# Strassen's products for the first four tiles of a pair's last phase, and the next batch's attention one step sooner there

## The chip, the cores and the metric

The kernel runs on one core of one Trainium2 chip. The metric is the device time of one execution in microseconds. In what follows PE is the TensorE engine with its matmuls, PEld its weight loads, DVE VectorE, ACT ScalarE, POOL GpSimd, and SP the engine that issues most of the transfers. Each of these works through its own instructions in the order in which the program wrote them.

## The reference

An attention block comes first. For 8 batches, 8 heads, 512 tokens and 32 state rows of 64 numbers each, it lets the tokens read from the states and the states read from the tokens. Its output, 544 rows of 512 numbers for each batch, goes through a feed-forward block with a cosine gate. Everything is float32.

```python
scores = scale * np.matmul(x, state.transpose(0, 1, 3, 2))
a = softmax(scores)                       # written out in the reference
xread = np.matmul(a, state)
scores2 = scale * np.matmul(state, x.transpose(0, 1, 3, 2))
a2 = softmax(scores2)
sread = np.matmul(a2, x)
x = concat([xread, sread], axis=2)        # to (4352, 512)
h = x @ w_in                              # 512 -> 2048
g = h * np.cos(h)
out = g @ w_out                           # 2048 -> 512
```

## The kernel before

**Tiles and steps.** The work is cut into tiles of 128 hidden units by 512 tokens: 16 tiles for each of 8 batches, and 16 more for the state rows at the end. A tile is one step of the loop at the end of the kernel function. The reads of the tokens are never formed: each batch's states are multiplied into `w_in` first (`products`, which PE writes to the PSUM tiles `at` and ACT copies to `sw`, L445), and the hidden values of a tile are then two products of 512 columns with the normalised weights `aT` (`hidden`, L471).

**Pairs and phases.** Two batches make a pair, and the product with `w_out` for a pair is done with Strassen's scheme over four phases. Phases 0 and 1 are the two halves of the 16 tiles of the even batch, phases 2 and 3 those of the odd batch. In phases 2 and 3 every tile also needs differences of `g` blocks (`sums`, `sums2`, L586): one for each tile on DVE, and in phase 3 two more on POOL. `output` (products at L624) follows a tile by three steps (`LAG`). In phase 3 it has four products of 512 columns for a tile, in phases 0 to 2 two, plus those that are left over from the pair before (`p7`, `p4`).

**Strassen in the hidden layer.** From batch 2 on, a predicate `seven` (L479) says for which tiles the hidden values of two neighbouring tiles are made together by seven products of 256 columns, in place of four products of 512 columns. `hidden_a` (four products, L514) is issued in the odd step before the pair, `hidden_b` (three products) in the pair's even step. Both take two fresh PSUM tiles `h` from a pool that has two. After `hidden_a`, ACT copies a part to the tile's place in `g_all` (L536), and DVE adds the rest (`sums_a`, L544 to L546). After `hidden_b` DVE adds again (`sums_b`, L559 and L560). The operands are differences that DVE makes once for each batch (`halves`, L493, to `aS`) and POOL for each pair of tiles (`sw_sums`, L509, four operations, to `swS` and into `sw`).

**The gate.** Every tile goes through four operations: `gate` (L567, ACT), `gate2` (L570, DVE), `gate3` (L573, ACT, a sine) and `gate4` (L580, DVE). A plain tile keeps its PSUM tile `h` until `gate4`. A tile made by Strassen's products leaves PSUM with the sums, and its gate reads `g_all`.

**The next batch's attention.** `plan(b)` writes down at which of the 16 steps of a batch each part of the next batch's attention goes in. `early` places the scores and row maxima (`scores` on PE, L319; `max1` on DVE, L333), their spread and the shift (L339, L356), the second maxima (`max2`, L349) and the exponentials (`exps` on ACT: L360 and twice L365, with a load of the activation table before and, at the next sine, after them), the sums (L333, L375, L376), their spread (L339), and the normalisation (`norm1`, L386). `late` places the turning of the weights (L392, copied by L397) and the reads (`reads`, L409). In the main loop a step's entries come in a fixed order: `hidden_b` and its sums, the next pair's `hidden_a`, go(0) (PE), `gate` and `gate2`, `sums_a`, go(1) and go(3) (the `x_` lists), `gate3`, `sw_sums`, `gate4`, the differences, go(2) and go(4) (the `y_` lists), and then the outputs. `exps` is in the list of go(4), so it stands at the end of its step on ACT.

Of the kernel before, what the change touches and what calls it, by code (L numbers as in the profile page):

```python
# [21 lines left out]
def kernel(  # L22
# [44 lines left out]
    NH = NF // 2  # L67
# [409 lines left out]


    def seven(t):  # L479
        return t.pair is not None and t.b > 1 and t.phase < 3  # L480

# [352 lines left out]
    def plan(b):  # L836
        pe, x_act, y_act, x_dve, y_dve = [
            {s: [] for s in range(NF)} for _ in range(5)]

        def prod(s, b, nt, *bank):  # L840
            pe[s].append((b, "products", nt) + bank)
            if b == 1 and 0 < nt < 3:
                x_dve[s].append((b, "products_taken", nt) + bank)
            else:
                x_act[s].append((b, "products_kept", nt) + bank)

        def pairs(s, b, name, kept, i):
            pe[s] += [(b, name, i), (b, name, i + 1)]
            x_act[s].append((b, kept, i))
            y_act[s].append((b, kept, i + 1))  # L850

        def early(b, s):
            if b == 1:
                pairs(s[0], b, "tokens", "tokens_kept", 0)
                pairs(s[1], b, "tokens", "tokens_kept", 2)
            else:
                for k in range(NK):
                    to = (x_dve, y_dve)[k % 2]
                    to[s[k // 2]].append((b, "tokens_turned", k))
            pe[s[2]].append((b, "scores"))  # L860
            x_dve[s[2]].append((b, "max1"))
            x_dve[s[3]].append((b, "spread1"))
            y_dve[s[3]].append((b, "shift"))
            x_dve[s[4]].append((b, "max2"))
            y_act[s[4]].append((b, "exps"))
            x_dve[s[5]].append((b, "sums"))
            y_dve[s[5]].append((b, "spread1"))
            x_dve[s[6]].append((b, "norm1"))

        def late(b, s):  # L870
            pairs(s[0], b, "turn", "turn_kept", 0)
            pe[s[1]].append((b, "reads", 0))
            pe[s[2]].append((b, "reads", 1))
            x_dve[s[2]].append((b, "keep"))
            if len(s) > 3:
                turned(b, s[3])

        def turned(b, s):
            pe[s].append((b, "keep2"))
            x_act[s].append((b, "keep3"))  # L880


        if b == 0:
            pe[0].append((0, "products", 0, SIDE, HC, WC))
            y_dve[0] += [(0, "products_taken", 0, SIDE, HC, WC),
                         (0, "inverse2")]
            prod(7, 0, 2, SIDE)
            prod(11, 0, 3)
            prod(13, 1, 0, MAIN)
            late(0, (1, 2, 3, 4))  # L890
            early(1, (5, 6, 7, 8, 9, 10, 11))
            late(1, (12, 13, 14))
        else:
            bank = (SIDE,) if b == 1 else ()
            if b == 1:
                turned(1, 0)
            prod(0, b, 1, *[MAIN for _ in bank])
            prod(4, b, 2, *bank)
            prod(9, b, 3, *bank)
            if b + 1 < B:  # L900
                prod(13, b + 1, 0)
                early(b + 1, (1 + (b == 1), 2 + (b == 1), 5, 6, 7, 8, 9))
                late(b + 1, (10, 11, 12, 15))
        return pe, x_act, y_act, x_dve, y_dve

# [21 lines left out]
    for step, t in enumerate(all_tiles):  # L927
        s = step % NF
        if s == 0 and t.b < B:
            steps = plan(t.b)  # L930
# [12 lines left out]
        if seven(t):  # L943
            if t.f % 2 == 0:
                hidden_b(t)
                sums_b(t)
                if s == NF - 2 and seven(all_tiles[step + 2]):
                    halves(t.b + 1)
        elif step != 1:
            hidden(t)  # L950
        first = len(ahead) > 1 and seven(ahead[0]) and ahead[0].f % 2 == 0
        if first:
            if not seven(t):
# [96 lines left out]
```

## Time and profile before

| what | us |
|---|---|
| median of 3 runs | 765.45 |
| lowest and highest of them | 764.82, 768.66 |
| profiled execution, own time | 765.96 |
| span in its profile | 764.2 |
| PE busy | 751.7 |
| DVE busy | 520.3 |
| ACT busy | 316.3 |
| POOL busy | 249.3 |

The span runs from the first to the last instruction of the profiled execution; what lies around it is the 1.8 us up to its own time. The granted TensorE clock is 0.997 of full speed. The starts of instructions are measured, the ends of matmuls are modelled, so neighbouring matmuls seem to overlap; what one costs on PE is read from start to start. In a list of groups the idle time behind the last bar is that of the engine ahead of those instructions, and the arrow names what ended it. L numbers are lines of the kernel before.

### The profile page before, as it was taken

Reading aid. Unit: us, or ns where it says so; the run is one execution under the profiler, and the core shown is the slowest. Engines: PE = TensorE matmul, PEld = TensorE weight load, DVE = VectorE, ACT = ScalarE, POOL = GpSimd, SP = SyncE. Lnnn points to the kernel's source line nnn. Section 1 sums busy time; section 2 is a strip of 40 time slices with the busy share of each in tenths; the row PEclk is TensorE's granted clock in tenths of the full one; section 3 lists DMA queues with packets and bytes.
Section 4 is the critical chain, followed back from the end, with each engine's and each line's share of the span. In section 5 each row is a group of like instructions: output and inputs, shape, how many; then the busy total and the mean of one; then the engine's idle time right before and its main releaser. Section 6 shows DMA issues by size and latency. Waiting matters only on the chain.

```text
span 764.2 us, 8416 instructions
## 1 busy us (share of the span) xinstructions
PE 751.7 (98%) x2880; PEld 380.4 (50%) x2880; DVE 520.3 (68%) x862; ACT 316.3 (41%) x523; POOL 249.3 (33%) x258
## 2 busy tenths in 40 slices
PE   8998999999999999999999999999999999999997
PEld 3443443445555554445555553445555554455554
DVE  5778777836896788847886789747878676432431
ACT  3887844533254335333362335333443333212212
POOL 2354278777121210662221111751211206500200
PEclk9999999999999999999999999999999999999999
DMA  8595461050002510340105210420100115000021
GB/s 247 170 274 209 131 98 29 4 107 1 14 15 49 90 28 4 54 82 0 29 1 97 41 28 15 70 54 1 27 1 1 28 28 138 0 0 15 14 42 41
DMA packets 161962, 43.54 MB, mean 57 GB/s; under 512 B 153920, under 2 KB 153920, under 8 KB 161920
## 3 DMA queue, kind: packets, MB, share of 16 engines
q1 hardware_dynamic: 161024, 42.49, 25.7%
q10 hardware_dynamic: 768, 0.39, 0.2%
q8 instruction: 23, 0.38, 0.2%
q14 instruction: 19, 0.16, 0.1%
q0 software_dynamic: 128, 0.13, 0.1%
HBM read 34.08 MB, written 8.91 MB: 56 GB/s over the span
## 4 chain that ended last, share of the span: by engine, by line
PE 87%; DVE 7%; ACT 2%; issue 1%; DMA 1%; POOL 1%; SPq 0%; DVEq 0%; ACTq 0%; POOLq 0%
PE o L624 47%; PE h L514 14%; PE h L471 14%; PE at L319 4%; PE o L744 4%; PE at L409 2%; DVE xT L339 1%; PE o L319 1%; DVE q L570 1%; DVE g_all L580 1%; DVE i L333 1%; DMA g_all<-in_moe_w_in_dram 1%; ACT q L567 1%; PE at L392 1%; DVE aT L356 1%
## 5 line engine op out<-in xcount | busy, mean ns | idle before, releaser
L624 PE MATMUL o<-g_all,w_out 128*128 128x512 f32 x512 | 236.4, 598 | 0.4 <-POOL w_out L242 0.4
L624 PE MATMUL o<-g_all,s 128*128 128x512 f32 x384 | 177.3, 598 | 0.0
L586 POOL TENSOR_TENSOR g_all<-g_all 128x512 f32<-128x512 f32 x80 | 112.8, 1433 | 121.2 <-DVE g_all L580 121.2
L624 PEld LDWEIGHTS o<-g_all,w_out 128*128 128x128 f32 x512 | 93.8, 190 | 113.1 <-issue 108.4
L573 ACT ACTIVATE q<-q,halfpi 128x512 f32<-128x512 f32 (+1 forms) x144 | 100.8, 700 | 95.8 <-DVE q L570 95.6
L624 PEld LDWEIGHTS o<-g_all,s 128*128 128x128 f32 x384 | 70.8, 190 | 88.1 <-issue 82.1
L570 DVE TENSOR_TENSOR q<-q,h 128x512 f32<-128x512 int32 (+1 forms) x69 | 42.9, 621 | 103.6 <-ACT q L567 103.6
L471 PE MATMUL h<-aT,sw 128*128 128x512 f32 x224 | 107.2, 602 | 4.8 <-DVE g_all L580 4.3
L567 ACT ACTIVATE q<-g_all 128x512 int32<-128x512 f32 x75 | 46.8, 624 | 141.8 <-DVE g_all L560 141.4
L567 ACT ACTIVATE q<-h 128x512 int32<-128x512 f32 (+1 forms) x69 | 37.6, 545 | 131.0 <-PE h L471 131.0
L570 DVE TENSOR_TENSOR q<-q,g_all 128x512 f32<-128x512 int32 x75 | 52.7, 703 | 35.5 <-ACT q L567 35.5
L471 PEld LDWEIGHTS h<-aT,sw 128*128 128x128 f32 x224 | 41.8, 190 | 60.2 <-issue 45.0
L509 POOL TENSOR_TENSOR swS<-sw 128x128 f32<-128x128 f32 x35 | 17.4, 496 | 148.6 <-PE h L514 107.3
L580 DVE TENSOR_TENSOR g_all<-g_all,q 128x512 f32<-128x512 f32 x75 | 54.0, 720 | 14.5 <-ACT q L573 14.4
L580 DVE TENSOR_TENSOR g_all<-h,q 128x512 f32<-128x512 f32 (+1 forms) x69 | 42.8, 621 | 23.5 <-ACT q L573 23.1
L242 POOL TENSOR_TENSOR w_out<-w_out,s 128x1024 int32<-128x1024 int32 x10 | 23.9, 2390 | 77.6 <-DVE w_out L237 73.4
L509 POOL TENSOR_TENSOR swS<-sw,swS 128x128 f32<-128x128 f32 x35 | 18.3, 522 | 87.4 <-PE h L514 86.9
L514 PEld LDWEIGHTS h<-aT,sw 128*128 128x128 f32 x144 | 27.4, 190 | 34.4 <-issue 28.0
L514 PE MATMUL h<-aS,sw 128*128 128x256 f32 x144 | 43.1, 381 | 0.1
L514 PE MATMUL h<-aS,swS 128*128 128x256 f32 x144 | 42.8, 379 | 0.0
L514 PE MATMUL h<-aT,sw 128*128 128x256 f32 x144 | 42.8, 379 | 0.0
L586 DVE TENSOR_TENSOR g_all<-g_all 128x512 f32<-128x512 f32 x48 | 33.5, 697 | 1.6
(107 smaller groups left out, 886.3 us busy)
## 6 DMA issues: line engine op xcount, KB each, us to landing
out_dram<-ot SPq DMA_DIRECT2D x132, 64.0 KB, 2.0
g_all<-in_moe_w_out_dram SPq DMA_DIRECT2D x8, 1024.0 KB, 5.0
g_all<-in_moe_w_in_dram SPq DMA_DIRECT2D x6, 1024.0 KB, 5.3
xT<-in_x_dram SPq DMA_DIRECT2D x96, 64.0 KB, 2.3
x_b<-in_x_dram SPq DMA_DIRECT2D x24, 256.0 KB, 4.5
x_b<-in_x_dram SPq DMA_DIRECT2D x16, 128.0 KB, 3.8
g_all<-in_moe_w_in_dram SPq DMA_DIRECT2D x4, 512.0 KB, 5.9
x_b<-in_moe_w_out_dram SPq DMA_DIRECT2D x1, 1024.0 KB, 6.1
```

Of the source, the lines that this page charges most:

```text
L242: nc.gpsimd.tensor_tensor(bits, bits, e, op=ALU.add)
L319: nc.tensor.matmul(out=(to or at)[j][Ns * k:Ns * k + Ns, 0:n], lhsT=w[D * j:D * j + D, self.b, Ns * k:Ns * k + Ns], rhs=r(slice(D * j, D * ...
L471: nc.tensor.matmul(out=t.hp, lhsT=t.lhs(i), rhs=t.rhs(i), start=(i == 0), stop=(i == t.kn - 1))
L509: engine.tensor_tensor(o, x1, x2, op=op)
L514: nc.tensor.matmul(out=out, lhsT=w, rhs=r, start=True, stop=True)
L567: nc.scalar.activation(t.q.bitcast(I32), t.hp, func=ACTF.Copy, bias=0.25)
L570: nc.vector.tensor_tensor(t.q, t.q.bitcast(I32), t.hp, op=ALU.subtract)
L573: nc.scalar.activation(t.q, t.q, func=ACTF.Sin, bias=halfpi, scale=-TWO_PI)
L580: nc.vector.tensor_tensor(t.g, t.hp, t.q, op=ALU.mult)
L586: engine.tensor_tensor(out, a, b, op=ALU.subtract)
L624: nc.tensor.matmul(out=acc[bank][ch], lhsT=w[:, i, P * ch:P * ch + P], rhs=g.g, start=(i == 0), stop=(i == NH - 1))
L744: nc.tensor.matmul(out=acc[MAIN][i], lhsT=t.g[:, P * i:P * i + P], rhs=w_out[:, :, t.f, :], start=(t.n_th == 0), stop=(t.n_th == NF - 1))
```

## The change

Strassen's products are extended to the first four tiles (`f` from 8 to 11) of phase 3. As the predicate also asks for a batch above 1, this concerns batches 3, 5 and 7. In the same batches the third block of products goes one step sooner (step 3 in place of 4), and for the next batch the five parts from scores to normalisation go one step sooner as well (scores 4, spread and shift 5, second maxima and exponentials 6, sums 7, normalisation 8). Batch 7 has no next batch.

```diff
     def seven(t):
-        return t.pair is not None and t.b > 1 and t.phase < 3
+        return t.pair is not None and t.b > 1 and (
+            t.phase < 3 or t.f < NH + 4)
...
             prod(0, b, 1, *[MAIN for _ in bank])
-            prod(4, b, 2, *bank)
+
+            soon = int(b % 2 == 1 and b > 1)
+            prod(4 - soon, b, 2, *bank)
             prod(9, b, 3, *bank)
             if b + 1 < B:
                 prod(13, b + 1, 0)
-                early(b + 1, (1 + (b == 1), 2 + (b == 1), 5, 6, 7, 8, 9))
+                early(b + 1, (1 + (b == 1), 2 + (b == 1)) + tuple(
+                    s - soon for s in (5, 6, 7, 8, 9)))
                 late(b + 1, (10, 11, 12, 15))
```

Everything that hangs on `seven` follows for those tiles: `hidden_a` and `hidden_b` with their sums in place of `hidden`, `sw_sums` for each pair of them, and gates that read `g_all`. The differences of phase 3 and the outputs stay as they were.

## The prediction

> **What bounds the kernel.** I read the shares by engine, then the groups by form, then the order of time around the last phase (steps 5 to 11 of batches 3, 5 and 7), and the busy time by stage there. From the page's shares:
>
> ```profile
> PE 751.7 (98%) x2880; PEld 380.4 (50%) x2880; DVE 520.3 (68%) x862; ACT 316.3 (41%) x523; POOL 249.3 (33%) x258
> ```
>
> and from the groups by form (busy us and mean ns of one between the bars, then idle time before them):
>
> ```profile
> L471 PE MATMUL h<-aT,sw 128*128 128x512 f32 x224 | 107.2, 602 | 4.8 <-DVE g_all L580 4.3 <-ACT sw L445 0.5
> ...
> L514 PE MATMUL h<-aS,sw 128*128 128x256 f32 x144 | 43.1, 381 | 0.1
> ```
>
> PE is busy 98%: what its columns cost, the kernel costs, and each wait of PE is added to the span. A product takes two records. The means overlap, so I price from start to start, in order of time (start, duration in us, engine, line; x4 merges four records):
>
> ```profile
> 296.52 1.88 PE L471 MATMUL h<-aT,sw 128*128 128x512 f32 x4
> ...
> 298.24 1.88 PE L624 MATMUL o<-g_all,s 128*128 128x512 f32 x4
> ...
> 369.01 0.59 PE L514 MATMUL h<-aT,sw 128*128 128x256 f32 x2
> ...
> 369.44 0.59 PE L514 MATMUL h<-aS,swS 128*128 128x256 f32 x2
> ```
>
> A plain tile (two products of 512 columns) takes 298.24 - 296.52 = 1.72; one Strassen product 369.44 - 369.01 = 0.43. Batch 3's last phase in the same view:
>
> ```profile
> 297.02 1.28 ACT L360 ACT_TABLE_LOAD   x1
> ...
> 298.31 1.06 ACT L360 ACTIVATE aT<-aT 128x1024 f32<-128x1024 f32 x1
> ...
> 300.60 0.59 ACT L567 ACTIVATE q<-h 128x512 int32<-128x512 f32 x1
> ...
> 304.95 1.98 PE L471 MATMUL h<-aT,sw 128*128 128x512 f32 x4 [0.18 <-DVE g_all L580]
> 304.98 3.01 POOL L586 TENSOR_TENSOR g_all<-g_all 128x512 f32<-128x512 f32 x2 [24.64 <-DVE g_all L580]
> ...
> 310.32 1.98 PE L471 MATMUL h<-aT,sw 128*128 128x512 f32 x4 [0.79 <-DVE g_all L580]
> ```
>
> The only PE waits of these stages are at the plain tiles: a tile's PSUM is free only after L580 of two tiles before. From start to start the two cost 0.35 and 0.95. Batch 5 has the same two (0.18, 0.79); batch 7, with no attention to prepare, none. Busy time by stage (PE, PEld, DVE, ACT, POOL) shows how little room DVE has:
>
> ```profile
> 283.70:288.36 4.66, 4.66 (x29) 2.38 (x28) 4.21 (x8) 0.99 (x2) 0.00 (x0) 1.00 0.32 50
> 288.36:296.52 8.16, 8.16 (x23) 4.18 (x22) 7.28 (x12) 2.11 (x4) 0.00 (x0) 1.00 0.00 0
> 296.52:304.95 8.43, 8.25 (x33) 2.95 (x31) 7.20 (x15) 8.10 (x13) 0.00 (x0) 1.00 0.01 2
> 304.95:312.23 7.28, 6.49 (x20) 2.94 (x21) 6.60 (x8) 2.40 (x4) 4.90 (x4) 1.00 0.41 66
> ```
>
> DVE works 25.3 of these 28.5 us; over the span it is at 68%.
>
> **What the skill says.** The Trainium skill, Perfetto Trace Analysis, "Tensor Engine Instruction (MATMUL, LD_WEIGHTS)": PE's end times are estimated, and ACT, DVE and GpSimd are strict FIFO. The trace agrees (0.59 records start 0.43 apart), and the order inside ACT and DVE decides below. ScalarE: Activation LUTs, "What ACT_TABLE_LOAD costs": about 1.283 us, and a drain of about 1.38 at every switch. The trace agrees on the load (1.28), not on the drain: L360 starts 0.01 after it.
>
> **The change, part by part.** Columns: a pair goes from 2 x 1.72 = 3.44 to 7 x 0.43 = 3.01, so -0.43; two pairs in each of batches 3, 5, 7: -2.6. The waits on L580 at steps 10 and 11 can go too, as these tiles leave PSUM by their sums: up to 2 x 1.3 = -2.6.
>
> Added on DVE, per pair: L544, L545, L546 (0.42, 0.42, 0.69) and L559, L560 (0.42, 0.68): 2.63, so 5.3 per batch. L570 and L580 read SBUF in place of PSUM at about 0.69 either way here.
>
> Added on ACT: one L536 (0.37) per pair. Added on POOL: four L509 (some 0.5 each), 2.0 per pair; POOL was idle for 24.64 us before its first subtraction of this phase, which hides them. Uncovered they would cost 2.0 a pair.
>
> Moved: products 2, scores and what follows, one step earlier. None issues a DMA, and SP's queue is unchanged; the token loads still hang on reads 1, unmoved. Scores go from 285.5 to about 280.3; their last transpose L301 began at 273.62, so nothing is late. The two L445 copies now stand before L573 of tile 3, about 0.5 late, hidden by L651, which holds DVE until 278.2.
>
> The parity is what costs. Exps go from the end of step 7 to the end of step 6. At step 7 ACT's next work is L536 of pair 8/9, now queued behind a table load (1.28), L360 and two L365 (2.29, from 298.31 to 300.60). Behind L536 wait sums_a on DVE, which frees the two PSUM buffers, and PE's second half of the pair.
>
> **The walk, batch 3,** on before's clock, each engine in its new order with durations and spacings of the rows above. Maxima, spread and shift (1.31, 1.24, 1.28) now stand ahead of step 6's sums_b.
>
> - DVE: L570 of tile 5 at 285.6 (before: 284.2; the maxima, 1.3, now go ahead of it), sums_a of 6/7 to 287.9 (PE needs it at 288.36: no wait), spread 287.9, L580 and L586 from 289.1, shift 290.4, sums_b 291.6 to 292.7 (before: 290.6). PE wants hidden_a of 8/9 at 293.1: no wait, by 0.4.
> - ACT: L567 of tile 6 at 292.8; DVE L570 at 293.5; L573 to 295.0, L567 of tile 7 to 295.6; table load to 296.9; exponentials to 299.2; only then L536, to 299.6. DVE: sums_a 299.65 to 301.3.
> - PE: hidden_b of 8/9 is wanted at 298.24. Its first product may start at 300.1, its second at 301.4 (0.85 after the first's end). **Wait 1: 2.7.**
> - DVE, in order, before sums_b of 8/9: sums (1.31 + 0.55), L580, L586 (1.3), spread (1.2), two L630 (1.25): sums_b starts at 306.9. PE, held till 301.4, has 0.86 of hidden_b and 1.72 of outputs left and is ready for hidden_a of 10/11 at 304.0. **Wait 2: 3.4.**
> - DVE: sums_b to 308.1, L567, L570 to 309.5, norm (1.2), L651, L580, L586, L570, sums_a of 10/11: 313.1 to 314.8. PE reaches hidden_b at 311.9 (1.72, products 1.02, outputs 1.72). **Wait 3: 2.5.**
> - Next late: turn_kept (L397) stands behind L567 of tile 10, which waits for its sums_b (317.8): reads 0 at 319.15, PE ready 318.5. **Wait 4: 0.65.** After that tiles are plain, steps are long and DVE catches up.
>
> Reads 0 start at 319.15 where before has 312.23: +6.9 for batch 3. The four waits are 9.3; less the 1.3 and the 0.86 that go, +7.1; the rest is rounding of switches between forms, and I take 7.0. Without the order, DVE's load alone says the same: to reads 0 it has 25.3 - 1.3 (maxima, gone ahead) + 4.2 (three of four sums) = 28.2 to do while PE has 28.5 - 2.2 = 26.3: at least 1.9 over, and idle times behind ACT come on top.
>
> Batch 5: same rows, +7.0. Batch 7: no attention, -0.43 x 2 = -0.9. Sum: +13.1. The profiled execution has a span of 764.2 and a time of 765.96, so these become 777.3 and 779.1. The median of the runs lies 0.5 below that time: 765.45 + 13.1 = 778.55, forecast **778.5 us**.
>
> The durations are those of rows of the same forms; unknown is how the three queues fall together. Below: no sum is late, -5.2. Above: the waits spill into the plain tiles, +20 (last rival). I take the walk, as each wait in it follows from an order that is fixed in the instruction streams.
>
> **Rivals.** *PE's columns decide, not slower.* Place: hidden_b of 8/9 in batches 3 and 5; it decides if sums_a ends by 298.2, where I have 301.3. For: even batches do all their attention beside Strassen's tiles, and PE has no wait there (batch 4's 367 to 392). Against: there L536 stands before the exponentials, and DVE has no L586 per tile. Price: -2.6 - 2.6 = -5.2: 760.3.
>
> *Only the order on ACT costs*, DVE catches up while PE waits: wait 1 stays, 2.7 - 1.3 - 0.86 = +0.5 in two batches, -0.9 in the third: 765.6. Against: after wait 1 DVE has 5.6 of work in a row before sums_b, and PE 3.0, so it holds only if half of that DVE work ran earlier.
>
> *The debt lasts* into steps 12 and 13 (halves and keep before L580 there): one more wait of about 3 in two batches: 784 to 786.
>
> That the change does not do what it says is out: the instruction stream has 42 more Strassen products and 24 fewer plain ones, six pairs.
>
> **How the numbers follow.** Walk 0.72 (770 to 784, the likeliest), ACT order alone 0.12, columns 0.10, debt 0.06. Range 765 to 784: it leaves out columns and debt, 0.16. A measurement here tells about 0.5% (3.8 us): faster is below 761.6, slower above 769.3. Faster 0.08 (columns), same 0.12 (ACT order, a milder columns case), slower 0.80.
>
> **What will show it.** Right: in batches 3 and 5, L514 waits on DVE L544 or L546 at step 8, on L560 at step 9, and an L536 that starts right after the second L365. L471's waits on L580 gone. Batch 7 shorter by 0.9, with no wait. Wrong: L536 before the exponentials, L514 records 0.43 apart through steps 7 to 10, or waits of PE on POOL L509 or DMA, which I priced at nothing.

## The result and the profile after

The changed kernel takes 786.35 us (median of 6 runs, 783.52 to 788.86); the kernel before, beside it, 765.67 (6 runs, 764.82 to 768.66). The ratio is 1.0266, with a 95% interval of 1.0237 to 1.0294: slower by 20.7 us, where 13.1 was forecast and 784 was the top of the range. The profiled execution took 786.77, its span is 785.0. From here on an operation is named by the line of the kernel after; up to L471 lines are as before, beyond that they are one higher (L580 of before is L581). In the kernels e13, e15 and e17 they are five higher still. Where the text takes up the forecast's own waits or terms, it keeps the forecast's line and says so.

Shares by engine, and two of the groups, of the kernel after:

```profile
PE 757.9 (97%) x2916; PEld 389.7 (50%) x2916; DVE 540.4 (69%) x892; ACT 318.8 (41%) x529; POOL 263.5 (34%) x282
...
L515 PE MATMUL h<-aT,sw 128*128 128x256 f32 x168 | 51.2, 387 | 9.9 <-DVE g_all L545 5.8
...
L625 PE MATMUL o<-g_all,s 128*128 128x512 f32 x384 | 180.9, 607 | 2.0 <-ACT held L636 2.0
```

PE has fewer columns to work and yet 6 us more busy time, in part from the half clock shown below. The groups show 9.9 us of idle time ahead of the first of Strassen's products in each half of a pair, where those of before show 0.1 at most, and one new wait on ACT. The waits of PE by line that it waited for (sum, times, longest):

```profile
PE h L515 <- DVE g_all L545: 5.8, 4, 2.2
PE h L515 <- DVE g_all L560: 4.0, 2, 2.9
PE h L515 <- DVE g_all L547: 3.5, 6, 0.6
PE h L471 <- DVE g_all L581: 2.4, 2, 1.9
PE o L625 <- ACT held L636: 2.0, 1, 2.0
```

The two waits on L581 that are left lie in the first two batches; those of the last phases are gone, as the forecast said, and the waits on L545, L547 and L560 stand in their place. To see where the time went, compare the starts of the same PE work in both traces: the second reads (L409) of each batch, and the first product of the state rows.

| stretch | forecast | measured |
|---|---|---|
| up to batch 2 | 0 | +0.2 |
| batch 3 | +7.0 | +8.5 |
| batch 4 | 0 | +0.3 |
| batch 5 | +7.0 | +7.45 |
| batch 6 | 0 | 0 |
| batch 7 | -0.9 | +4.3 |
| sum | +13.1 | +20.8 |

Of the 7.7 that the forecast is short, batch 7 has 5.2. Batch 3's last phase in order of time (start, duration, idle time before and what ended it in brackets):

```profile
299.31 0.37 ACT L537 COPY g_all<-h 128x256 f32<-128x256 f32 x1
...
299.70 0.42 DVE L545 TENSOR_TENSOR g_all<-g_all,h 128x256 f32<-128x256 f32 x1 [1.82 <-ACT g_all L537]
...
300.18 0.70 PE L515 MATMUL h<-aT,sw 128*128 128x256 f32 x2 [1.55 <-DVE g_all L545]
...
301.52 0.67 PE L515 MATMUL h<-aT,swS 128*128 128x256 f32 x2 [0.64 <-DVE g_all L547]
...
302.52 3.51 PE L625 MATMUL o<-g_all,s 128*128 128x512 f32 x4
...
307.21 0.70 PE L515 MATMUL h<-aT,sw 128*128 128x256 f32 x2 [1.17 <-DVE g_all L560]
...
311.60 3.45 POOL L587 TENSOR_TENSOR g_all<-g_all 128x512 f32<-128x512 f32 x2 [8.40 <-DVE g_all L581]
...
312.17 1.75 DVE L571 TENSOR_TENSOR q<-q,g_all 128x512 f32<-128x512 int32 x1
...
314.30 0.70 PE L515 MATMUL h<-aT,sw 128*128 128x256 f32 x2 [2.17 <-DVE g_all L545]
...
315.64 0.83 PE L515 MATMUL h<-aT,swS 128*128 128x256 f32 x2 [0.64 <-DVE g_all L547]
...
320.94 1.10 PE L409 MATMUL at<-x_b,xT 128*64 128x128 f32 x16
```

The first six lines are the walk's waits 1 and 2: the copy L537 starts only at 299.31, as the last exponential ends, DVE has idled 1.82 for it, and PE follows. Two things are not in the walk. At 302.52 four records take 3.51 where they took 1.88 before: PE runs at half its clock there. And the second gate operation L571 takes 1.75 at 312.17, where rows of its form took 0.69 before. Batch 7 in the same view:

```profile
653.31 3.45 POOL L587 TENSOR_TENSOR g_all<-g_all 128x512 f32<-128x512 f32 x2 [3.15 <-DVE g_all L581]
...
653.88 1.76 DVE L571 TENSOR_TENSOR q<-q,g_all 128x512 f32<-128x512 int32 x1
...
657.35 0.67 PE L515 MATMUL h<-aT,swS 128*128 128x256 f32 x2 [0.64 <-DVE g_all L547]
...
663.21 0.57 ACT L636 ACTIVATE held<-o 128x512 f32<-128x512 f32 x1
...
663.84 3.48 PE L625 MATMUL o<-g_all,s 128*128 128x512 f32 x4 [1.95 <-ACT held L636]
```

L571 again takes 1.76 as soon as POOL's subtractions L587 have started, and PE waits 0.64 for the sums behind it. Then the outputs wait 1.95 for L636, the copy of a finished output on ACT, which stands behind the gates of both tiles of the pair; and a stretch at half clock follows. The granted clock is the last but two of these columns (stretch, its length, busy time of PE, PEld, DVE, ACT, POOL, clock, DMA share, GB/s):

```profile
299.00:306.00 7.00, 5.18 (x10) 2.19 (x10) 6.06 (x11) 2.68 (x5) 0.87 (x2) 0.76 0.00 1
...
316.00:320.00 4.00, 4.00 (x15) 2.99 (x14) 2.93 (x6) 1.10 (x2) 3.01 (x2) 0.57 0.43 68
480.00:490.00 10.00, 7.04 (x30) 3.38 (x28) 9.21 (x13) 3.20 (x6) 2.26 (x2) 0.83 0.16 25
...
660.00:668.00 8.00, 6.05 (x11) 2.36 (x10) 5.60 (x8) 3.07 (x5) 5.26 (x5) 0.79 0.85 241
```

There are four such stretches, of 3.41 us each, against one in the kernel before (early, at 73.7), the last microseconds of either span left aside; in each, PE does half of the 3.41, so 1.7 us of its work is put off.

### The profile page after: what moved, and what is told of

Read it like the earlier page. It is cut to its first block, busy times and chain, and to the rows that moved or that the text cites. A ratio compares the mean times of both kernels' runs of the same rounds, so it can differ in the third digit from the quotient of the medians.

```text
span 785.0 us, 8565 instructions
## 1 busy us (share of the span) xinstructions
PE 757.9 (97%) x2916; PEld 389.7 (50%) x2916; DVE 540.4 (69%) x892; ACT 318.8 (41%) x529; POOL 263.5 (34%) x282
## 4 chain that ended last, share of the span: by engine, by line
PE 80%; DVE 12%; ACT 3%; DMA 2%; issue 2%; POOL 0%; ACTq 0%; DVEq 0%
PE o L625 43%; PE h L515 13%; PE h L471 12%; PE at L319 4%; PE o L745 4%; PE at L409 2%; DVE q L571 2%; DVE g_all L581 1%; DVE xT L339 1%; ACT q L568 1%; PE o L319 1%; DMA g_all<-in_moe_w_out_dram 1%; PE o L802 1%; DVE g_all L587 1%; DVE i L333 1%
## 5 line engine op out<-in xcount | busy, mean ns | idle before, releaser
L587 POOL TENSOR_TENSOR g_all<-g_all 128x512 f32<-128x512 f32 x80 | 115.6, 1467 | 74.9 <-DVE g_all L581 74.9
L568 ACT ACTIVATE q<-g_all 128x512 int32<-128x512 f32 x87 | 54.2, 623 | 172.9 <-DVE g_all L561 172.5
L571 DVE TENSOR_TENSOR q<-q,h 128x512 f32<-128x512 int32 (+1 forms) x57 | 34.7, 609 | 95.7 <-ACT q L568 95.7
L571 DVE TENSOR_TENSOR q<-q,g_all 128x512 f32<-128x512 int32 x87 | 66.9, 769 | 40.3 <-ACT q L568 40.3
L471 PE MATMUL h<-aT,sw 128*128 128x512 f32 x176 | 83.4, 597 | 2.9 <-DVE g_all L581 2.4
L510 POOL TENSOR_TENSOR swS<-sw 128x128 f32<-128x128 f32 x41 | 20.0, 487 | 176.6 <-PE h L515 136.7
L568 ACT ACTIVATE q<-h 128x512 int32<-128x512 f32 (+1 forms) x57 | 30.5, 535 | 116.9 <-PE h L471 116.9
L581 DVE TENSOR_TENSOR g_all<-g_all,q 128x512 f32<-128x512 f32 x87 | 62.5, 718 | 17.8 <-ACT q L574 17.7
L515 PE MATMUL h<-aT,sw 128*128 128x256 f32 x168 | 51.2, 387 | 9.9 <-DVE g_all L545 5.8
L510 POOL TENSOR_TENSOR swS<-sw,swS 128x128 f32<-128x128 f32 x41 | 20.4, 499 | 110.8 <-PE h L515 110.3
L471 PEld LDWEIGHTS h<-aT,sw 128*128 128x128 f32 x176 | 33.1, 192 | 46.1 <-issue 36.3
L515 PE MATMUL h<-aS,sw 128*128 128x256 f32 x168 | 51.3, 387 | 0.1
L515 PE MATMUL h<-aS,swS 128*128 128x256 f32 x168 | 50.8, 384 | 0.0
L581 DVE TENSOR_TENSOR g_all<-h,q 128x512 f32<-128x512 f32 (+1 forms) x57 | 34.7, 608 | 17.8 <-ACT q L574 15.9
L515 PEld LDWEIGHTS h<-aS,sw 128*128 128x128 f32 x168 | 32.2, 193 | 5.6 <-issue 0.7
```

The source lines that it names most:

```text
L471: nc.tensor.matmul(out=t.hp, lhsT=t.lhs(i), rhs=t.rhs(i), start=(i == 0), stop=(i == t.kn - 1))
L510: engine.tensor_tensor(o, x1, x2, op=op)
L515: nc.tensor.matmul(out=out, lhsT=w, rhs=r, start=True, stop=True)
L568: nc.scalar.activation(t.q.bitcast(I32), t.hp, func=ACTF.Copy, bias=0.25)
L571: nc.vector.tensor_tensor(t.q, t.q.bitcast(I32), t.hp, op=ALU.subtract)
L581: nc.vector.tensor_tensor(t.g, t.hp, t.q, op=ALU.mult)
```

## The experiments

Three questions: which part of the change costs what (e1 to e3), where the exponentials may stand (e4, e8, e12), and what of DVE, POOL and the clock makes PE wait (all others). The kernel before ran beside each: 766.0 to 766.2.

| kernel | us | ratio, 95% interval |
|---|---|---|
| changed kernel | 786.35 | 1.0266, 1.0237 to 1.0294 |
| e1 Strassen's tiles without the move | 779.23 | 1.0163, 1.0134 to 1.0191 |
| e2 the move without the tiles | 773.4 | 1.0085, 1.0061 to 1.0108 |
| e3 the tiles in batch 7 alone | 769.11 | 1.0041, 1.0030 to 1.0051 |
| e4 changed, exponentials back at step 7 | 778.83 | 1.0158, 1.0128 to 1.0188 |
| e8 the move by two steps, no tiles | 765.68 | 1.0001, 0.9992 to 1.0009 |
| e12 half of the move, no tiles | 768.38 | 1.0033, 1.0021 to 1.0045 |
| e5 as e3, POOL's subtractions later | 768.03 | 1.0029, 1.0017 to 1.0042 |
| e9 as e3, without POOL's subtractions | 767.01 | 1.0016, 1.0008 to 1.0025 |
| e6 changed, POOL's subtractions later | 783.77 | 1.0231, 1.0215 to 1.0247 |
| e7 as e6, moved by two steps | 780.69 | 1.0194, 1.0180 to 1.0208 |
| e10 as e1, less subtraction on DVE | 774.0 | 1.0107, 1.0093 to 1.0120 |
| e11 changed, less subtraction on DVE | 777.72 | 1.0153, 1.0138 to 1.0168 |
| e13 tiles in 3 and 5, normalisation later | 774.07 | 1.0113, 1.0094 to 1.0132 |
| e15 as e13, sums ahead of the gate | 773.15 | 1.0089, 1.0071 to 1.0108 |
| e17 as e13, less subtraction on DVE | 763.64 | 0.9968, 0.9956 to 0.9980 |
| e14 before, normalisation later | 763.39 | 0.9964, 0.9953 to 0.9976 |
| e16 changed, PE's waits filled | 786.15 | 1.0252, 1.0230 to 1.0274 |

The medians mix executions with more and with fewer stretches at half clock. So here are the stages of the profiled executions as well, each against before and measured as in the last table (us; batches 4 and 6 stay within 0.4). The last column gives the stretches at half clock in batches 3, 5 and 7.

| kernel | batch 3 | batch 5 | batch 7 | half clock in |
|---|---|---|---|---|
| changed kernel | +8.5 | +7.45 | +4.3 | 3 (twice), 5, 7 |
| e1 | +4.55 | +4.55 | +4.3 | 5, 7 |
| e2 | +3.5 | +3.55 | 0 | 3, 5 |
| e3 | 0 | 0 | +2.8 | none |
| e9 | 0 | 0 | +1.2 | none |
| e10 | +2.3 | +1.9 | +3.2 | 3 |
| e11 | +3.7 | +3.7 | +4.5 | 7 |
| e13 | +2.8 | +2.4 | 0 | none |
| e17 | -1.3 | -1.3 | 0 | none |
| e14 | -1.5 | -1.5 | 0 | none |
| e16 | +7.5 | +7.5 | +4.5 | 7 |

### e1, e2, e3: the parts of the change

```diff
 e1, against after
-            soon = int(b % 2 == 1 and b > 1)
+            soon = 0
 e2, against after
-            t.phase < 3 or t.f < NH + 4)
+            t.phase < 3)
 e3, against before
-        return t.pair is not None and t.b > 1 and t.phase < 3
+        return t.pair is not None and t.b > 1 and (
+            t.phase < 3 or t.b == B - 1 and t.f < NH + 4)
```

> Strassen's products for tiles 8 to 11, the attention at its old steps. Queue-order theory: the exponentials stand at the end of step 7 again, behind the copy of pair 8/9, so the wait of 2.5 us at step 8 and the stretch at half clock behind it (1.7 us) go in batches 3 and 5; the load of DVE and batch 7's 4.3 us stay: 776 to 780 us. Rival, DVE's load alone: the same sums have to be done in the same time, so the wait only moves: 785 to 788 us.

> The attention one step sooner in batches 3, 5 (and products 2 in 7), no further Strassen tiles. Queue-order theory: a plain tile has no copy behind the exponentials, and the two waits on L580 of batches 3 and 5 (1.3 us each) shrink at most: 763 to 766 us. Rival, the move itself is what costs (maxima, spread and shift ahead of step 6's sums): 770 us or more.

> Strassen's products for tiles 8 to 11 in batch 7 alone, which prepares no attention; nothing moved. The prediction's step for batch 7: 0.9 us less, 764.8 us. Theory from the trace of after: L571 reads both operands from SBUF while POOL subtracts and takes 1.2 to 1.8 us in place of 0.7, the sums are late, and the copy of the first output (L636) behind them holds PE: 4.3 us more, 770 us.

The tiles alone cost 13.2 us (779.23 - 766.04), the move alone 7.4, batch 7's tiles alone 3.1. 13.2 + 7.4 is 20.6: the parts add to what the whole change costs, 20.7. So the move is about a third, and the tiles in batches 3 and 5, with their attention where it always was, together with batch 7 take the rest. By the medians that rest is 10.1 and 3.1. By the stages it is 9.1 for batches 3 and 5, and for batch 7 it is 2.8 without a stretch at half clock (e3) and 4.3 with one (e1, whose code for batch 7 is that of e3, and the changed kernel). The move costs without any tile of the change, which the forecast had not thought of, and e2 came out in the range of its rival; e2 in order of time:

```profile
299.22 1.28 ACT L574 ACT_TABLE_LOAD   x1
...
300.52 0.72 ACT L574 ACTIVATE q<-q,halfpi 128x512 f32<-128x512 f32 x1
...
301.27 0.69 DVE L581 TENSOR_TENSOR g_all<-g_all,q 128x512 f32<-128x512 f32 x1 [1.38 <-ACT q L574]
...
308.00 3.31 PE L471 MATMUL h<-aT,sw 128*128 128x512 f32 x4 [3.08 <-DVE g_all L581]
...
308.02 5.91 POOL L587 TENSOR_TENSOR g_all<-g_all 128x512 f32<-128x512 f32 x4 [26.85 <-DVE g_all L581]
...
308.59 0.68 DVE L571 TENSOR_TENSOR q<-q,h 128x512 f32<-128x512 int32 x1
```

Here the exponentials and the table load hold the sine of tile 7 until 300.52, DVE idles 1.38 for it at L581, and everything behind is late: PE waits 3.08 two steps on. The last line is of use below: with `h` in PSUM, L571 takes 0.68 though POOL has been busy since 308.02.

### e4, e8, e12: where the exponentials stand

```diff
 e4, against after
-            y_act[s[4]].append((b, "exps"))
+            y_act[s[5] - 1].append((b, "exps"))
...
-                    s - soon for s in (5, 6, 7, 8, 9)))
+                    s - soon * (s < 8) for s in (5, 6, 7, 8, 9)))
 e8, against before: soon = 2 * int(b % 2 == 1 and b > 1), and
-                early(b + 1, (1 + (b == 1), 2 + (b == 1), 5, 6, 7, 8, 9))
+                early(b + 1, (1 + (b == 1) - soon // 2, 2 + (b == 1) - soon // 2) + tuple(
+                    s - soon for s in (5, 6, 7, 8, 9)))
 e12, against before: e4's placing, soon = int(b % 2 == 1 and b > 1)
```

> After, with the exponentials, sums and normalisation left at their old steps 7, 8, 9; scores, maxima, spread and shift one step sooner as in after. Queue-order theory: the copy of pair 8/9 stands ahead of the exponentials; the wait of 2.5 us and the half-clock stretch behind it go in batches 3 and 5: about 8 us less than after, 777 to 779 us. Rival, DVE's load alone: 785 to 788 us.

> Before, with the attention two steps sooner in batches 3 and 5, no further Strassen tiles, POOL as before. Parity theory: the exponentials at the end of an odd step hold up no tile's gate in the middle of a pair, so the 7.4 us that one step sooner costs are absent: 763 to 767 us. Rival, attention ahead of its place costs whatever the step: 772 us or more.

> Before, with only scores, maxima, spread, shift and second maxima (and products 2) one step sooner in batches 3 and 5; exponentials, sums and normalisation at their old steps; no further Strassen tiles. Theory: the two waits on L580 at steps 10 and 11 (1.3 us a batch) go as DVE has less left there: 763 to 764.5 us. Rival: the debt only moves, 765.5 to 767 us.

With the exponentials, the sums and the normalisation back at steps 7, 8 and 9 and all the rest moved, the changed kernel takes 778.83, the time of e1 (779.23): what costs in the move is the exponentials at the end of an even step, with the sums and the normalisation that were moved along with them. Two steps sooner they stand at the end of an odd step again, and the move costs nothing (765.68 against 766.02). Moving only what stands ahead of them gains nothing either: 768.38, above both of the ranges expected; PE's waits on L581 in batch 3 became 1.19 and 0.79, from 0.18 and 0.79. That part of my theory fell. Without the tiles, then, the later part of the move makes 5.0 of its 7.4 us (773.4 - 768.38); the 2.4 of the earlier part were not followed further.

### e10, e11, e13, e14, e15, e17: DVE's work and its order

e10 (against e1) and e11 (against after) leave out DVE's subtraction for tiles 4 to 11 of batches 3 and 5:

```diff
-        if t.phase == 2:
+        if t.phase == 2 and not (t.b in (3, 5) and i > 3):
...
-            minus(pr, pr.b[0, i].g, t.g, pr.b[0, i].g, True)
+            if not (t.b in (3, 5) and i < 4):
+                minus(pr, pr.b[0, i].g, t.g, pr.b[0, i].g, True)
```

> As the run with Strassen's tiles and the attention at its old steps (779.2 us), with DVE's subtraction left out for tiles 4 to 11 of batches 3 and 5 (8 x 0.69 = 5.5 us of DVE work per batch, about what the sums of these tiles add; part of the output blocks is incomplete). DVE-load theory: the 10 us that batches 3 and 5 cost go, batch 7's 3 us stay: 767 to 770 us. Rival, the order of the queues and the chain between ACT and DVE cost it: 775 us or more.

> After, with the same subtractions of DVE left out in batches 3 and 5. If the exponentials ahead of the copy are a cause of their own, the wait on L545 at step 8 stays (2.5 us, with or without half clock behind it) in both batches: 772 to 777 us. If DVE's load is all of it: 767 to 770 us.

e13 keeps all work and moves the attention's sums, their spread and the normalisation from steps 8 and 9 to 11 and 12, behind Strassen's pairs; the spread then goes into the buffer `aS`, which is free by that time, and the next `halves` two steps later. It has the tiles in batches 3 and 5 only, and the rest as before. e14 is the kernel before with that later place alone. e15 is e13 with `sums_a` ahead of `gate2` in the last phase. e17 is e13 with the omission of e10.

```diff
 e13 and e14
-            y_dve[s[5]].append((b, "spread1"))
+            y_dve[s[5]].append((b, "spread2" if s[5] > 10 else "spread1"))
...
-                early(b + 1, (1 + (b == 1), 2 + (b == 1), 5, 6, 7, 8, 9))
+                early(b + 1, (1 + (b == 1), 2 + (b == 1), 5, 6, 7) + (
+                    (11, 12) if b % 2 == 1 and b > 1 else (8, 9)))
 e15, against e13
+            early_sums = first and ahead[0].phase == 3
+            if early_sums:
+                sums_a(ahead[0])
             gate2(t)
...
-            if first:
+            if first and not early_sums:
                 sums_a(ahead[0])
```

> Strassen's tiles 8 to 11 in batches 3 and 5 alone (batch 7 as before); the attention at its old steps up to the exponentials (end of step 7), but sums, spread and normalisation at steps 11 and 12 in place of 8 and 9, and the differences of the next pair (halves) at step 13; the spread goes to another buffer that is free then. Local-load theory (what DVE has to do between the sums of one pair and of the next costs these batches their time): without those 4.4 us there, PE keeps its 0.86 us a batch and loses the waits of before in part: 762 to 766 us. Rival, the serial chain of a pair's gate between ACT and DVE is too long in this phase whatever else DVE does: 770 us or more.

> Before, with only that later place for sums, spread, normalisation and halves in batches 3 and 5; no further Strassen tiles. Local-load theory: the two waits on L580 at steps 10 and 11 (1.3 us a batch) go: 763 to 764 us. Rival: 765.5 us or more.

> The kernel with Strassen's tiles in batches 3 and 5 alone and the attention's sums and normalisation later (774.07), with one order changed on DVE: in the last phase the sums of the coming pair's first half (sums_a) stand ahead of the second gate operation (gate2) of the odd tile before them, in place of behind it. No work is added or left out. Theory of the serial chain: there gate2 of the odd tile takes 1.76 from 306.73 and sums_a starts only at 308.41, so PE waits 1.89 at step 10; with sums_a at 306.7 that wait falls to about 0.2, the 0.99 for its last sum stays, and each of batches 3 and 5 is shorter by 1.7: 774.07 - 3.4 = 770.7, 769 to 772. Rival, the amount of DVE work decides and its order does not: gate2 is pushed back, the next sums are late by as much, 773 to 775.

> The kernel with Strassen's tiles in batches 3 and 5 alone and the attention's sums and normalisation later (774.07), with DVE's subtraction for tiles 4 to 11 of batches 3 and 5 left out as well: eight of 0.69 per batch, 5.5 us of DVE's work; the differences that the outputs use are then those of older values. Theory, the amount of DVE's work in these steps is all of the cost: with the attention's 4.9 moved out and 5.5 left out, DVE has less to do than in the kernel before, nothing of the cost is left and the columns show: PE's 0.86 per batch and the waits of 1.3 go, 762 to 765. If the two reliefs only add as they measured alone (5.2 and 2.1 of the 10.1 that these two batches cost): 768.8. Rival, what is left is the serial way from sums through gate, table load, sine and gate2 beside GpSimd, which no relief of DVE shortens: 768 to 772.

e10 takes 5.2 us off e1, e13 takes 2.1 off the 10.1 of these two batches by the medians, 3.9 off 9.1 by the stages. Its runs scatter most: three take 771.4 to 772.8 at a granted clock of 0.996 to 0.998, the profiled one among them, and three 775.4 to 776.7 at 0.989 to 0.991. e10 fell between what its two theories gave, e13 in the range of its rival (770 or more), the serial chain. From e13's trace I took that chain up: a serial way would decide, not an amount. In e13 (L576 is `gate2`, L550 the first sum, L520 Strassen's product) `gate2` of the odd tile stood between:

```profile
306.73 1.76 DVE L576 TENSOR_TENSOR q<-q,g_all 128x512 f32<-128x512 int32 x1
...
308.41 0.41 DVE L550 TENSOR_TENSOR g_all<-g_all,h 128x256 f32<-128x256 f32 x1
...
308.87 0.70 PE L520 MATMUL h<-aT,sw 128*128 128x256 f32 x2 [1.89 <-DVE g_all L550]
...
314.79 1.09 PE L414 MATMUL at<-x_b,xT 128*64 128x128 f32 x16 [0.54 <-ACT xT L402]
```

e15 puts the sum first, and that wait goes as expected, but another grows:

```profile
308.21 0.70 PE L520 MATMUL h<-aT,sw 128*128 128x256 f32 x2 [0.21 <-DVE g_all L550]
...
315.39 1.09 PE L414 MATMUL at<-x_b,xT 128*64 128x128 f32 x16 [2.15 <-ACT xT L402]
```

1.68 less at L550, 1.61 more at the reads, whose turned weights (L402) stand behind a gate that is now later; 773.15 against 774.07 is within the intervals, and in batch 5, where neither trace has a stretch at half clock, the stage is +2.4 in both. The rival had it: this order on DVE moves the wait along, it doesn't pay it. e17 then shows what does. With both reliefs these batches are faster than before, 763.64 for the kernel, well below the 768.8 of reliefs that only add, and of PE's waits there only this is left (sum, times, longest; L552 is the last of the sums):

```profile
PE h L520 <- DVE g_all L552: 1.0, 2, 0.5
```

Against e14, which has no tiles and all of DVE's work, the tiles still cost 0.2 a batch. So the cost of the tiles in these batches follows the DVE work in these steps. The two reliefs also shorten the queue of DVE ahead of the sums, so they don't tell the amount of work from the length of that queue; e15 is the only run that changes the order alone. From the second half of pair 6/7 to the first reads of batch 3, by start times and busy time within them:

| kernel | length, us | DVE busy, us | DVE busy, share |
|---|---|---|---|
| before | 23.87 | 21.08 | 0.88 |
| after | 32.37 | 26.84 | 0.83 |
| e1 | 28.41 | 25.25 | 0.89 |
| e10 | 26.18 | 22.56 | 0.86 |
| e13 | 26.63 | 22.47 | 0.84 |
| e14 | 22.37 | 18.57 | 0.83 |
| e17 | 22.31 | 18.04 | 0.81 |

In e14 PE is busy for all of the 22.37; from before to e13, where PE waits, the stretch is DVE's busy time and 12 to 21% on top, which is DVE's idle time; in e17 PE waits only 0.5. The busy time of DVE includes what L571 loses beside POOL, more than 1 us in the rows of after and e13. e10 and e13 have the same 22.5 of work by quite different edits, and the same length within 0.5. e11's 777.72 agrees in kind, just above the range expected if the order is a cause of its own: 8.6 off the changed kernel, 1.4 to 1.8 a batch above e10, and the wait on L545 at step 8 is smaller (0.69 in place of 1.55) but still there, where e1 has none.

e14 is the best version of all: the kernel before with the attention's sums and normalisation after the plain tiles. 763.39, 0.36% faster than before and faster than both kernels, by less than the 0.5% that I set as the bound of a change but with an interval that lies below one. PE's waits on the fourth gate operation (L581 of after) in batches 3 and 5 are gone there, and DVE has 2.5 less to do in the tight stretch.

### e5, e9, e3 again, e6, e7: POOL's subtractions

e5 and e6 issue POOL's two subtractions of tiles 8 to 11 three steps later, with the tile's output; e9 leaves those of batch 7 out; e7 is e6 with the move by two steps as in e8.

```diff
 e5 against e3, e6 against after
-            minus(pr, pr.b[2, i].g, t.g, pr.b[2, i].g)
+            if not seven(t):
+                minus(pr, pr.b[2, i].g, t.g, pr.b[2, i].g)
...
-        if t.phase == 3:
+        if t.phase == 3 and not seven(t):
...
+        for u in line[:1]:
+            if len(line) >= LAG and u.phase == 3 and seven(u):
+                sums_later(u)
 e9, against e3: the first two of these, without sums_later
```

> As the run with Strassen's tiles in batch 7 alone (769.1 us), but POOL's two subtractions for each of tiles 8 to 11 are issued three steps later, away from the gates of these tiles. Contention theory (L571 with both inputs in SBUF waits for POOL's subtraction): L571 back at 0.7 us, the waits on L545 and L547 gone, and 764 to 765.5 us, the prediction's -0.9. If only the place of L636 on ACT matters: 767 us. Rival, the sums are late whatever POOL does: 769 us.

> Strassen's tiles in batch 7 alone, with POOL's two subtractions for tiles 8 to 11 of batch 7 left out altogether (so the second halves of the last pair are incomplete). Contention theory: every L571 there at 0.7 us, no wait on L545 and L547 at step 10; if L636 then comes in time, 764 to 765 us, if its place on ACT behind the gates still holds PE by 1 us or more, 766 to 767 us. Rival, the sums are late without POOL too: 768 to 769 us.

> After, with POOL's subtractions for tiles 8 to 11 three steps later in batches 3, 5 and 7. Contention theory: 3 to 4 us less in batch 7, and in batches 3 and 5 the 1.1 us that L571 of tile 9 loses, with the waits that follow from it: 777 to 781 us. Rival, POOL matters in batch 7 alone: 782 to 783 us.

> After, but the attention two steps sooner in batches 3 and 5 (exponentials at the end of step 5, an odd step, behind the copy of pair 6/7; products 2 at step 2, scores at 3), and POOL's subtractions three steps later. Parity theory: the exponentials no longer stand between a pair's copy and its sums, and DVE's work is spread over more steps: 763 to 768 us. Rival, DVE's load alone: 774 us or more.

Without POOL's subtractions beside them all of L571 in batch 7 are back at 0.68 or 0.69, PE's waits on L545 and L547 there are gone, and of the 3.1 us of e3 there is 1.0 left (767.01), by the stages 1.2 of 2.8. What remains is the wait for the output's copy, in e9:

```profile
PE o L625 <- ACT held L636: 1.4, 1, 1.4
```

Issued later (e5), POOL still ran beside an L571 (1.76 again), and a third of the cost went by the medians, 0.5 of 2.8 by the stages. e6 gained 2.6, less than either range said, and batch 7 has 2.0 of it in the trace: 4.3 went to 2.3, with no stretch at half clock there. In its batch 3 an L571 still takes 1.76 at 312.19, so e6 doesn't settle POOL's part in batches 3 and 5. e1's trace does: in its batch 3 no L571 ahead of the reads takes more than 0.69 but one of 0.94, and the batch costs 4.55. With the exponentials at an odd step as well (e7) batches 3 and 5 still cost 6.2 each, in the range of its rival: neither POOL nor the order was the main thing there.

### e16: does the half clock cost time?

```diff
+    def fill(t, n):
+        for _ in range(n):
+            product_of(at[0][:, LO], blocks_of(t)[0], aT_of[t.b][:, 0, LO])
...
             if t.f % 2 == 0:
+                if t.phase == 3 and t.b < B - 1:
+                    fill(t, 3)
                 hidden_b(t)
...
+            if t.f == NH + 1 and t.phase == 3 and t.b < B - 1:
+                fill(ahead[0], 6)
             hidden_a(*ahead)
```

> The changed kernel with idle time of PE filled in the last phases of batches 3 and 5: ahead of the second half of pair 8/9 three more products of 256 columns (0.43 us each, 1.29), ahead of the first half of pair 10/11 six (2.57), ahead of its second half three (1.29), all into a score bank that is free then and that nobody reads. The output is whole. The profile of the changed kernel has PE at half clock for 3.41 us after 302.4, 316.0 and 483.3, each right after such waits, and 1.7 of work is lost in each. Theory A, the clock adds its loss to the time: without idle time before them the three stretches go, 786.35 - 5.1 = 781.2, 780 to 782.5. Theory B, the chain of DVE and ACT sets the end of these stages and PE's slow stretches lie in time that it would have waited: in batch 3 the stretch is followed by a wait on L560 of 1.17 where batch 5, which has no stretch there, waits 2.87; in batch 5 the next stretch is followed by a wait on L545 of 0.55 where batch 3 waits 2.17. Only the one after 316.0 counts, up to 1.4: 785, 784 to 787.

With idle time taken up by products that nobody reads, the clock stays at full speed in all three places and only batch 7's stretch is left (columns as above):

```profile
299.00:306.00 7.00, 6.35 (x24) 4.41 (x25) 5.83 (x11) 2.90 (x5) 0.87 (x2) 1.00 0.00 1
306.00:316.00 10.00, 8.19 (x43) 4.55 (x42) 9.07 (x14) 3.83 (x7) 3.45 (x2) 1.00 0.18 29
316.00:320.00 4.00, 3.57 (x16) 2.11 (x16) 2.93 (x6) 1.04 (x2) 2.99 (x2) 1.00 0.43 68
480.00:490.00 10.00, 8.84 (x47) 5.38 (x45) 9.11 (x13) 3.81 (x7) 3.06 (x2) 1.00 0.17 28
```

The time stays too: 786.15 against 786.35, in the range of theory B. The product after the fill starts at 307.43 where it started at 307.21. By the stages the two stretches of batch 3 cost 1.0 together (8.5 went to 7.5), and that of batch 5 nothing (7.45 and 7.5): for the most part PE's slow stretches there lie in time that it would have waited for DVE anyway. Theory A, that each adds its 1.7, has fallen for these three. Batch 7's stretch was not filled, and there it does cost: the stage takes 4.3 to 4.5 in the five traces that have it (the changed kernel, e1, e4, e11, e16), and 2.8 and 3.2 in e3 and e10, which have none. For batch 7, e1, e3 and e10 are the same code; the others have one block of products a step sooner, which costs nothing there (e2).

## Why the prediction was right and wrong

**Right: the direction, and the mechanism of batches 3 and 5.** In the forecast's lines: the waits on L580 left; those on L544 and L546 came (L545 and L547 of after), and at step 9 one on L559 (L560 of after), the sum just ahead of the one named; and the copy L536 (L537 of after) starts right after the second L365, at 299.31. Wait 1 was forecast at 2.7; in the trace the starts are 1.72 + 0.80 = 2.5 late. Wait 2, forecast 3.4, is 2.87 in batch 5; in batch 3 the half clock uses up 1.7 of it and 1.17 is left. Wait 3, forecast 2.5, is 2.17 + 0.64 in batch 3, and 0.55 + 0.64 in batch 5, where PE came later; about 1.1 of it is what L571 loses beside POOL (1.75 at 312.17), which the walk doesn't have, so that it is so near is in part luck. Wait 4, forecast 0.65, is at most 0.26. The batches came to +8.5 and +7.45 where the walk has +7.0; with PE's waits filled (e16) both come to +7.5. The walk's own cross-check from DVE's load was the sounder half of it: e10, e13 and e17 show that the cost follows this load.

**Wrong: "Batch 7: no attention, -0.43 x 2 = -0.9", with no wait.** It came to +4.3, which is 5.2 of the 7.7 us that the forecast was short. The term that failed is "L570 and L580 read SBUF in place of PSUM at about 0.69 either way". For L580 (L581 of after) it holds roughly, 0.65 to 0.89; L570 (L571 of after), the gate's second operation, takes 1.75 or 1.76 when POOL's subtraction has just started, and 0.94 to 1.23 later in it, in the changed kernel. I had seen POOL's row and asked only whether POOL was late. The Trainium skill states the rule, SBUF — State Buffer, "Who interferes with whom" and "SBUF: two separate sides": a VectorE instruction with two SBUF inputs and a GpSimd instruction that reads SBUF need the same pair of ports, held for a whole instruction, while the other waits. The trace agrees on both sides: 1.75 with both inputs in SBUF, 0.68 beside POOL with one in PSUM (e2), 0.68 and 0.69 with POOL's work left out (e9). It is about 2.1 of the 3.1 us that batch 7's tiles cost alone (769.11 - 767.01), by the stages 1.6 of 2.8. The rest was not in the sum at all: L636 on ACT stands behind the second tile's L568, which in a pair made by Strassen's products hangs on the last sums. This 1.0 is what e9 has left, though the columns alone should give 0.9 less; that L636 causes it is read from the order on ACT and its wait of 1.42 and was not tried by itself, and where the few tenths beyond that wait go stays open. The other 1.5, from 2.8 to 4.3, go with the stretch at half clock that follows the wait on L636 in the changed kernel: the same wait of 1.95 has no such stretch behind it in e3.

**Wrong in weight: "The parity is what costs."** It does cost, and moving the exponentials back to an odd step by one (e4) or on by one (e8) takes its price away. But it is 7.4 of 20.6. With the attention where it was, the tiles cost 13.2; the forecast gave no number for that kernel, but its chain of waits has no first link there. I let the one fixed order that I had found carry the whole sum, while the load that I had counted beside it (28.2 of work for 26.3 of PE) holds without it all the more. The rivals *PE's columns decide* and *only the order on ACT costs* are both refuted by e1, which has the columns without that order and costs 4.55 in each of batches 3 and 5. *The debt lasts* gave 784 to 786, close to the result, but for a reason that isn't there: no wait stands at steps 12 and 13.

**Right, at nothing: POOL's L509 (L510 of after), the scores' earlier place, SP's queue.** No wait of PE stands on any of them.

**The columns themselves.** In e17, where DVE is relieved, PE pays 0.43 a product as forecast, and waits 0.51 per batch on the last sum. The stretch is 22.31 long where e14's plain tiles take 22.37, and by the end of the batch it is 0.2 behind e14, so even with the cover given nothing of the 0.86 per batch is left.

The granted clock, which the forecast did not mention, is the smaller part of the miss: by the stages 1.0 in batch 3 and 1.5 in batch 7, 2.5 of the 7.7 us.

## What to carry to other kernels

Count an added operation against the engine's load in that stage, with the idle times behind its partners: here DVE never got above 89% busy in the tight stretch, and from e17 to e1, 7.2 us more of its busy time made the stretch 6.1 us longer. When operands move from PSUM to SBUF, look at what GpSimd does at that moment before calling it even. An order changed on a full engine can lengthen the stage (e2) or move the wait to the next consumer (e15); what shortened it here was work taken out of it (e14, e17).

## What the hardware showed that I had not expected

- A subtraction on DVE of 128x512 with both operands in SBUF took 1.75 us in place of 0.69 when GpSimd's subtraction of 128x512 had started 0.6 us ahead of it; with one operand in PSUM it took 0.68 in the same situation.
- The granted clock of PE fell to 0.5 for 3.41 us at a time, after less idle time than such a stretch is long. The Trainium skill, TensorE: Matmul & The Clock Gate, "What's actually happening", gives a free-running window of 3413 ns, which agrees in length, and an idle window as the condition, which these waits do not fill. In each trace the changes of the clock lie whole multiples of 3.413 us apart. Counted in such steps, by the profile's busy time and from 20 to 750 us in the traces of before, after and e1 to e17, each of the 24 steps at full speed in which PE was idle for 1.94 us or more was followed by a stretch at half clock, and none in which it was idle for less than 1.66; between the two both occur. So it matters how a wait falls on the steps: the 2.88 of e1 in batch 3 falls into two, with 1.87 and 1.65 of idle time in them, and no stretch follows; the same wait in batch 5 puts 2.71 into one, and one does. Filled with products (e16), none came.
- A half-clock stretch can cost nothing, where PE would have waited for another engine next (batch 5: 7.45 with it, 7.5 with the waits filled); in batch 7, where it would not, it went with 1.5 us.
